# Banded attention and a gated FFN on one core: the fifth block of queries goes over to the 32-query form, in an order of work made anew

## The chip, the cores and the metric

One core of a Trainium2 chip runs the whole program. The metric is device time in microseconds (us), the median of a few executions of the same program. The engines are named as the profile names them: PE is TensorE's matmuls, PEld its weight loads, DVE is VectorE, ACT is ScalarE, POOL is GpSimd, SP is SyncE, which issues nearly all DMAs.

## The reference

The input is q, k, v of shape (8, 8, 576, 64) (batch, heads, sequence, head size) and two weight matrices, 512x2048 and 2048x512, all as drawn in float32 (the weights are handed over as 64-bit numbers).

```
scores = q @ k^T / sqrt(64)             # a query sees its own key and the 63 before it
attn   = softmax(masked scores)         # per head and batch
x      = (attn @ v), heads side by side # 4608 tokens x 512
h      = x @ w_in                       # 4608 x 2048
g      = h if h >= 1, 0 if h <= -1, else (h + 1)^2 / 4
out    = g @ w_out                      # 4608 x 512
```

## The kernel before, in words

**Tiles.** The 4608 tokens are nine tiles of 512 tokens. The attention works in steps of 128 queries (all 8 heads), four steps to a tile, 36 in all; the FFN of a tile loops over 16 blocks f of 128 hidden units. Tiles 0 to 2 are done plainly: `ffn_in` (L1147) makes h in PSUM with three fp32r products (high by high, high by low, low by high), `ffn_relu`, `ffn_square`, `ffn_gate` make g, `ffn_high` and `ffn_low` split it again, `ffn_out` (L1187) adds it to the output. Tiles 3 to 8 are three pairs that share sums of blocks, with seven products in place of eight (`ffn_product` L921, `out_product` L1007). Those pairs read weight sums that `add_sums` (L866) makes beside tiles 1 and 2, and operands that `add_build` (L644) makes from the attention of the pair.

**Weights.** Each block of weights comes as raw 64-bit words by DMA (`w_load`, L304). Five passes on ACT and DVE (L311 to L358) turn it into a high and a low fp32r part. This work fills ACT and DVE through most of tile 0.

**Attention, three forms.** `att_scores` (L426) makes the scores of a step on PE, two PSUM banks.
- Steps 0 to 3 (`PE_MASKS`): 64 queries with 128 keys; PE adds the mask; DVE takes the maximum; ACT takes the exponential; DVE inverts and normalizes; PE transposes (`att_transpose_pe`, L533), eight 128x128 transposes; ACT or DVE copies the two results out of PSUM (`att_transposed`, L539); `att_values` (L542) multiplies by v.
- Step 4 is the same, but DVE adds the mask (L469) and takes the maximum in a second pass (L473).
- Steps 5 and on (s >= `SOON`): 32 queries with 96 keys. `att_masked` (L455) adds the mask and takes the lowest in one pass of eight small instructions (L462); the exponentials are L482; one normalization for both halves (L501); one 32x32-wise transpose on DVE in place (`att_turn`, L506); two DMA writes to the tile moved in DRAM (`att_write`, L517) and one DMA read back into ptd (`att_read`, L521), which leaves the block as `att_values` wants it.

The first step of the last form needs parts of moved to be zero: `att_clear` (L510) on POOL clears a part of ptd, after the values of all steps of the older forms (`early_values`, L627) have been made, since these use the same tile; two DMAs (`att_zero`, L513) write the zeros. There is one such tile ptd for a step (`pt2`) and one moved, so a step's writes wait for the read of the step before, and a step's read waits for the values of the step before.

**The order of the work.** Nothing is ordered by hand, instruction by instruction. Each piece of work is given to `Plan` (L128) with a key, a cost per engine, what it waits for and the buffers that it takes and gives. `Plan.run` goes through the pieces and gives each engine, whenever it is free, the piece that could start first, by least key among those that could (`PATIENCE`, L100, widens this for ACT and POOL). The order that comes out is the program order of each engine and of SP's DMA queue. The keys are in units of one block f for 384 tokens (`step`, L1232; a tile of 512 tokens is 21.33 units). The constants of L33 to L125 set keys and costs: `A_FIRST`, `A_LEAD`, `A_STEP` for the scores, `D_LATE` and `B_DUE` for what follows them, `W_FIRST`, `W_STEP`, `W_LATE` for the weights, `W0_KEY` and `L_LEAD` for loads, `S_LATE` and `S_PACE` for weight sums, `BUILD` for operands. The due times that `soon` (L1235) gives say when a step of tile 1 is wanted. Tile 1 begins with halves of 256 tokens (`FRONT`, L1245): its first half needs steps 4 and 5, its second half steps 6 and 7.

Of the kernel before, what the change touches and what calls it, by code (L numbers as in the profile page):

```python
# [34 lines left out]

PE_STEPS = 5
PE_MASKS = 4
LENT = 2
FIRST = 4
SOON = 5  # L40
JOIN = 8
BEHIND = 2
E_SPAN = 0.29
E_LEAD = 9.81
W_LEAD = -1.5
W_FIRST = (17.22, -2.0, 1.41, 1.48, -3.05)
W_STEP = 1.02
L_LEAD = -0.77
W_LATE = (3.72, -1.06, -2.67, 7.19, 13.28, 13.03, 18.55)
W_LOAD = 1400  # L50
Q_LOAD = 700
K_LOAD = 1040
V_LATE = 2.92
W0_KEY = -100.2
FIRST_LOAD = 0, (0,)
M_LATE = 1
W0_STEP = 12.29
FINE = 4
NWARM = 8
A_FIRST = (-102.6, -95.58, -95.43, -95)  # L60
A_NEXT = 1.57
A_STEP = 4.75
A_SPAN = 2.18
A_LEAD = 4.64
O_LAG = 2.79
O_LAG_DMA = 2300
DMA_LAG = 1300
# [10 lines left out]
B_PE = 2210  # L78
B_DUE = (2.44, -1.28, -0.74)
B_STEP = 5.68  # L80
B_FIRST = 1.45
A_END = 5.86
V_PE = 1270
NORM = dict(Pool=800, DVE=480), dict(DVE=610)
G_LATE = (1.94, 1.65, -4.21, -4.45, 2.08)
D_LATE = (-0.7, 0.46, 6.3, -3.34, 6.37, 0.12)
TURN = 965, 1500
# [5 lines left out]
K_LAG = 4500  # L93
# [4 lines left out]
SUM_KEEP = 1150  # L98
V_LATE_2 = 14.69
PATIENCE = dict(ACT=300, DVE=0, Pool=303, PE=0, SP=0)  # L100
# [5 lines left out]
SUPERS = 3  # L106
H_STEP = 18.67
S_LATE = 1.62
S_PACE = 2.47
O_CHANGE = 3.33, 3.2, 4.7  # L110
EARLY_2 = 2.71
A_SUPER = ((7.71, 2.68), (9.52, 4.03))
A_ORDER = (0, 4, 1, 5, 2, 6, 3, 7)
BUILD = (-12.04, 16.74)
X_SLOTS = 4, 0, 6, 1, 2, 3
# [3 lines left out]
WRITES = (1, None), (2, 1), (0, None), (3, 2), (3, 3), (1, 2), (2, 2)  # L119
R_LEAD = -4.99  # L120
R_LOAD = 430
L_DVE = 4, 6, 8
G_LEAD = (3.99, -2.67, 0.94, -2.12)
OP_LEAD = 10.45
D_LEAD = 0.72  # L125


class Plan:  # L128
# [10 lines left out]
    def add(self, key, cost, do, after=(), takes=(), gives=(), lag=0, shared=False):  # L139
        self.work.append((key, cost, do, set(after), takes, gives, lag, shared))  # L140
        return len(self.work) - 1
# [77 lines left out]
def banded_attention_then_ffn(ctx: ExitStack, tc: tile.TileContext, q, k, v, w, masks, out, out_t, dims):  # L219
# [65 lines left out]
    add = plan.add  # L285
# [76 lines left out]
    def add_weights(f, units):  # L362
        g = f, units
        m = len(units) * DM
        act, high, join, low, small = 105 + .916 * m, 92 + .844 * m, 10 + 1.22 * m, 67 + 1.05 * m, 90 + .25 * m
        key = f * W_STEP - (W_FIRST[f] if f < len(W_FIRST) else W_LEAD) + .5 * units[0]
        x = add(W0_KEY + W0_STEP * (f + .5 * units[0]), dict(SP=W_LOAD * len(units)), lambda e: None if g == FIRST_LOAD else w_load(g), lag=DMA_LAG)
        xr = add(key - W_LATE[0], dict(ACT=act), lambda e: w_rest(g), [x], takes=["u"])
        x = add(key, dict(ACT=act), lambda e: w_sign(g), [xr])
        x = add(key - W_LATE[1], dict(DVE=small), lambda e: w_limit_signed(g), [x])  # L370
        x = add(key - W_LATE[2], dict(DVE=small), lambda e: w_limit_unsigned(g), [x])
        x = add(key - W_LATE[3], dict(DVE=small), lambda e: w_shift(g), [x])
        x = add(key - W_LATE[4], dict(DVE=join), lambda e: w_join(g), [x])
# [294 lines left out]
    def add_step(t, i):  # L668

        s = starts[t] // SB + i  # L670
# [5 lines left out]
        if s < FIRST:  # L676
            key = due = A_FIRST[s]
        elif s >= JOIN:
            key = a_keys[s]
        else:  # L680
            key = a_keys[s]
            due = min(key + A_SPAN, soon(s))
        lk = key - L_LEAD
        apart = A_SUPER[t > PLAIN][1]
        if s == 0:
            last["r"] = add(lk, dict(ACT=480), lambda e: round_masks())
        if s == PE_STEPS - 2:
            last["m"] = add(lk + M_LATE, dict(SP=590), lambda e: load_masks(), lag=DMA_LAG)
        late = s >= JOIN
        xq = add(lk, dict(SP=Q_LOAD), lambda e: load_q(s), takes=["qt"], lag=Q_LAG if late else DMA_LAG)  # L690
        xk = add(lk, dict(SP=Q_LOAD if late else K_LOAD), lambda e: load_k(s) if s else None, takes=["kt"], lag=K_LAG if late else DMA_LAG)
        vk, vl = lk + (V_LATE_2 if late else V_LATE), V_LAG if late else DMA_LAG
# [58 lines left out]
        else:  # L751
            dk = key if s >= JOIN else min(key + E_SPAN, soon(s) - E_LEAD)
            due = [dk + B_DUE[0], dk + B_DUE[0] + B_DUE[2]]
            x = [add(due[h], dict(DVE=LOWEST), lambda e, h=h: att_masked(s, h), [xs, last["m"]], gives=[(ps, xs, h)]) for h in range(2)]
            x = [add(due[h], dict(ACT=EXP[1]), lambda e, h=h: att_exp(s, h, False), [x[h]]) for h in range(2)]
            x = add(due[1], dict(DVE=430), lambda e: att_inverse(s, BOTH), x)
            x = [add(due[1], dict(DVE=870, Pool=1650) if s >= JOIN else dict(DVE=870), lambda e: att_normalize(s, BOTH, e), [x], shared=True)]
            due = dk + B_DUE[1]
            if s == SOON:
# [444 lines left out]
    def out_late(t, q, i):  # L1204
        if t < PLAIN - 1 or q < NF - 2:
            return O_LAG
        return O_CHANGE[0] if q == NF - 2 else O_CHANGE[1 + i // 2]
# [219 lines left out]
```

## Time and profile before

| what | us |
|---|---|
| median of 3 runs | 840.63 (839.79 to 840.87) |
| the profiled execution, its time | 843.4 |
| its span, first to last instruction | 841.6 |
| PE busy in the span | 821.6 |
| DVE busy | 687.0 |
| ACT busy | 533.5 |
| POOL busy | 213.8 |

The profiled execution is one further run of the same program. Its own time is 1.8 us more than its span, which leaves out what lies before the first and after the last instruction, and 2.8 us more than the median of the runs. Its mean granted TensorE clock is 0.994 of 2.4 GHz. Matmul ends are modelled, so two matmuls of a run overlap in the timeline: the cost of one is read from start to start.

### The profile page before, as it was taken

Reading aid. Unit: us, or ns where it says so; the run is one execution under the profiler, and the core shown is the slowest. Engines: PE = TensorE matmul, PEld = TensorE weight load, DVE = VectorE, ACT = ScalarE, POOL = GpSimd, SP = SyncE. Lnnn points to the kernel's source line nnn. Section 1 sums busy time; section 2 is a strip of 40 time slices with the busy share of each in tenths; the row PEclk is TensorE's granted clock in tenths of the full one; section 3 lists DMA queues with packets and bytes.
Section 4 is the critical chain, followed back from the end, with each engine's and each line's share of the span. In section 5 each row is a group of like instructions: output and inputs, shape, how many; then the busy total and the mean of one; then the engine's idle time right before and its main releaser. Section 6 shows DMA issues by size and latency. Waiting matters only on the chain.

```text
span 841.6 us, 18582 instructions
## 1 busy us (share of the span) xinstructions
PE 821.6 (98%) x6588; PEld 672.1 (80%) x6588; DVE 687.0 (82%) x1613; ACT 533.5 (63%) x1303; POOL 213.8 (25%) x226
## 2 busy tenths in 40 slices
PE   7889999999999999999999999999999999999998
PEld 5767788878787878788888888888888888888886
DVE  6999996468757789888899986888999848878964
ACT  5999983545654764756775654777756536566442
POOL 1000014335664636221233320122332201100100
PEclk8999999999999999999999999999999999999999
DMA  8994359996788797788898898888888877777775
GB/s 322 394 375 170 100 165 331 362 331 200 214 265 262 219 285 235 271 252 272 272 333 253 284 316 281 269 268 282 302 252 244 294 230 198 192 195 193 198 224 164
DMA packets 151901, 216.08 MB, mean 257 GB/s; under 512 B 11904, under 2 KB 75264, under 8 KB 151808
## 3 DMA queue, kind: packets, MB, share of 16 engines
q1 hardware_dynamic: 151520, 213.97, 80.2%
q8 instruction: 53, 0.87, 0.4%
q10 hardware_dynamic: 288, 0.92, 0.3%
q14 instruction: 40, 0.33, 0.1%
HBM read 163.72 MB, written 51.12 MB: 255 GB/s over the span
## 4 chain that ended last, share of the span: by engine, by line
PE 75%; DVE 10%; DMA 7%; ACT 3%; issue 2%; POOL 2%; SPq 1%; ACTq 0%; POOLq 0%; DVEq 0%
PE acc L1014 27%; PE ps_h L928 14%; PE acc L928 14%; PE ps_h L1153 8%; PE acc L1199 7%; DMA kept<-u 4%; PE ps_a L439 2%; DVE u L842 1%; PE ps_a L552 1%; DVE u L857 1%; PE ps_h L552 1%; DVE u L849 1%; DMA raw<-in_w 1%; DVE wts L358 1%; DMA kt<-in_k 1%
## 5 line engine op out<-in xcount | busy, mean ns | idle before, releaser
L1014 PE MATMUL acc<-op,wts 128*128 128x512 f32 x576 | 137.7, 390 | 0.0
L1153 PE MATMUL ps_h<-xh,wts 128*128 128x512 f32 (+1 forms) x424 | 131.2, 376 | 6.1 <-DVE a L1175 4.4
L290 ACT CAST op<-g 128x512 fp32r<-128x512 f32 x129 | 80.2, 622 | 77.4 <-PE acc L1014 49.3
L1014 PEld LDWEIGHTS acc<-op,wts 128*128 128x128 f32 x576 | 107.8, 188 | 22.5
L1199 PE MATMUL acc<-wts,gh 128*128 128x512 f32 x384 | 120.1, 394 | 0.7 <-ACT gh L1180 0.7
L482 ACT ACTIVATE sm<-sm,nm 128x96 f32<-128x96 f32 x248 | 89.5, 363 | 12.3 <-DVE nm L462 11.6
L1153 PEld LDWEIGHTS ps_h<-xh,wts 128*128 128x128 f32 x424 | 78.0, 190 | 22.6 <-DVE a L1175 6.5
L1005 DVE TENSOR_TENSOR op<-g,op 128x512 fp32r<-128x512 f32 x107 | 76.7, 718 | 20.7 <-ACT op L290 20.2
L928 PE MATMUL ps_h<-wts 128*128 128x512 f32 x360 | 92.0, 391 | 0.0
L928 PE MATMUL acc<-wts 128*128 128x512 f32 x360 | 91.5, 389 | 0.0
L1199 PEld LDWEIGHTS acc<-wts,gh 128*128 128x128 f32 x384 | 70.8, 188 | 16.0 <-ACT gh L1180 1.1
L1168 ACT ACTIVATE a<-a 128x512 f32<-128x512 f32 (+1 forms) x125 | 77.1, 617 | 3.8
L1153 PE MATMUL ps_h<-xl,wts 128*128 128x512 f32 (+1 forms) x212 | 78.8, 372 | 0.6 <-DVE xl L565 0.6
L928 PEld LDWEIGHTS acc<-wts 128*128 128x128 f32 x360 | 67.5, 188 | 14.2
L928 PEld LDWEIGHTS ps_h<-wts 128*128 128x128 f32 x360 | 67.2, 188 | 14.2
L1199 PE MATMUL acc<-wts,gl 128*128 128x512 f32 x192 | 75.3, 392 | 1.4 <-DVE gl L1185 1.4
L1163 ACT ACTIVATE a<-g 128x512 f32<-128x512 f32 x96 | 60.5, 630 | 19.4 <-DVE g L943 14.0
L1175 DVE SCALAR_TENSOR_TENSOR g<-a,g 128x512 f32<-128x512 f32 x96 | 68.1, 716 | 3.8 <-ACT a L1168 3.2
L1005 POOL TENSOR_TENSOR op<-g,op 128x512 fp32r<-128x512 f32 x28 | 36.1, 1295 | 129.5 <-ACT op L290 118.1
L1185 POOL TENSOR_TENSOR gl<-a,gh 128x512 fp32r<-128x512 f32 (+1 forms) x34 | 48.6, 1429 | 45.0 <-ACT gh L1180 43.2
L992 DVE TENSOR_TENSOR g<-g 128x512 f32<-128x512 f32 x83 | 58.4, 717 | 0.5
L1175 DVE SCALAR_TENSOR_TENSOR a<-a,ps_h 128x512 f32<-128x512 f32 (+1 forms) x53 | 33.3, 628 | 25.1 <-ACT a L1168 24.9
(145 smaller groups left out, 1544.5 us busy)
## 6 DMA issues: line engine op xcount, KB each, us to landing
wts<-kept SPq DMA_DIRECT2D x240, 256.0 KB, 3.6
vt<-in_v SPq DMA_DIRECT2D x72, 256.0 KB, 4.9
ptd<-moved SPq DMA_DIRECT2D x31, 512.0 KB, 4.7
kt<-in_k SPq DMA_DIRECT2D x35, 384.0 KB, 5.1
kept<-wts SPq DMA_DIRECT2D x48, 256.0 KB, 4.8
gh<-kept SPq DMA_DIRECT2D x48, 256.0 KB, 3.7
gl<-kept SPq DMA_DIRECT2D x48, 256.0 KB, 3.6
raw<-in_w SPq DMA_DIRECT2D x12, 1023.8 KB, 10.6
```

The costliest lines, as they stand in the source:

```text
L290: nc.scalar.copy(dst, src)
L482: nc.scalar.activation(t, t, AF.Exp, bias=nm[:, g:g + 1], scale=-1.0, accum_out=den[:, g:g + 1])
L928: nc.tensor.matmul(ps, lhsT=r[:, part, cp], rhs=x_op(k, xp)[:, cp], start=j in (0, 1, 3, 4) and i == 0 and cp == 0, stop=j in (1, 2, 5, 6) ...
L992: engine[eng].tensor_tensor(out=g[:, out], in0=g[:, a], in1=g[:, b], op=op)
L1005: engine[eng].tensor_tensor(out=low, in0=g_of(n)[:, of], in1=high.bitcast(F32), op=ALU.subtract)
L1014: nc.tensor.matmul(opened[b][m], lhsT=r[:, part, m], rhs=op[xp], start=j in (0, 1, 3, 4) and i == 0 and n == 0, stop=j in (1, 2, 5, 6) and ...
L1153: nc.tensor.matmul(ps, lhsT=wts[f, 0][:, part, c * P:(c + 1) * P], rhs=x[:, c, r], start=(c == 0 and j == 0), stop=(c == NP - 1 and j == 2),)
L1163: nc.scalar.activation(gs[t, f, r.start][0], phs[t, f, r.start], AF.Relu, bias=0.5, scale=0.5)
L1168: nc.scalar.activation(a, a, AF.Square)
L1175: nc.vector.scalar_tensor_tensor(out=ps if t >= PLAIN else a, in0=a, scalar=1.0, in1=ps, op0=ALU.min, op1=ALU.max)
L1185: engine[eng].tensor_tensor(out=g[2], in0=g[0], in1=g[1].bitcast(F32), op=ALU.subtract)
L1199: nc.tensor.matmul(acc[t, i][:, n], lhsT=g[:, sub], rhs=wts[f, 1][:, part, n], start=(q == 0 and j == 0), stop=(q == NF - 1 and j == 2 and ...
```

## The change

Step 4 goes over to the form of steps 5 and on: `PE_STEPS` and `SOON` are 4 in place of 5. So its scores are 32 smaller products in place of 16, the second maximum pass, the eight PE transposes and the two copies fall away, and one DVE transpose, two DMA writes and one DMA read are added. `att_clear` and `att_zero` belong to step 4 now and wait for the values of steps 0 to 3; the mask load belongs to step 2. The constants of the order are new throughout, and some have new companions: `A_SHIFT` moves the due times of steps 0 to 7 one by one, `L_LEAD_1` and `B_DUE_1` stand for the steps before step 8, `O_LAG_1` for tile 0; `AHEAD` puts the first q load, the first k load and the first weight load ahead of all others (the last two are issued from ACT already).

```diff
@@ -33,36 +33,40 @@
 FRONT = 2
 BACK = 1
 
-PE_STEPS = 5
+PE_STEPS = 4
 PE_MASKS = 4
 LENT = 2
 FIRST = 4
-SOON = 5
+SOON = 4
 JOIN = 8
 BEHIND = 2
-E_SPAN = 0.29
-E_LEAD = 9.81
-W_LEAD = -1.5
-W_FIRST = (17.22, -2.0, 1.41, 1.48, -3.05)
-W_STEP = 1.02
-L_LEAD = -0.77
-W_LATE = (3.72, -1.06, -2.67, 7.19, 13.28, 13.03, 18.55)
+E_SPAN = 6.84
+E_LEAD = 3.34
+W_LEAD = -1.6
+W_FIRST = (15.88, -1.61, 3.35, 3.69, -1.83, -1.49, -1.81, -2.17, -1.35, -1.5, -1.09, -0.24, -0.95, -2.54)
+W_STEP = 1.23
+L_LEAD = 0.75
+L_LEAD_1 = -2.65
+W_LATE = (5.04, -3.82, -1.64, 5.78, 15.71, 7.97, 16.52)
 W_LOAD = 1400
 Q_LOAD = 700
 K_LOAD = 1040
-V_LATE = 2.92
-W0_KEY = -100.2
+V_LATE = 5.42
+W0_KEY = -104.03
 FIRST_LOAD = 0, (0,)
-M_LATE = 1
-W0_STEP = 12.29
+M_LATE = 4.03
+AHEAD = -10000
+W0_STEP = 12.28
 FINE = 4
 NWARM = 8
-A_FIRST = (-102.6, -95.58, -95.43, -95)
-A_NEXT = 1.57
-A_STEP = 4.75
-A_SPAN = 2.18
-A_LEAD = 4.64
-O_LAG = 2.79
+A_FIRST = (-106.83, -104.6, -94.45, -93.06)
+A_SHIFT = (-5.96, -4.16, -2.18, 1.29, -0.01, 2.05, -4.27, 2.83)
+A_NEXT = 2.2
+A_STEP = 5.3
+A_SPAN = 20.93
+A_LEAD = 0.18
+O_LAG = 3.7
+O_LAG_1 = 1.81
 O_LAG_DMA = 2300
 DMA_LAG = 1300
 BEGIN = dict(PE=1500, ACT=2300, DVE=2500, SP=2400)
@@ -76,14 +80,15 @@
 EXP = 1545, 1440
 S_PE = 1230, 1150
 B_PE = 2210
-B_DUE = (2.44, -1.28, -0.74)
-B_STEP = 5.68
-B_FIRST = 1.45
-A_END = 5.86
+B_DUE = (-1.05, 0.05, 0.26)
+B_DUE_1 = (2.86, 0.39, -3.32)
+B_STEP = 6.97
+B_FIRST = 1.97
+A_END = 4.22
 V_PE = 1270
 NORM = dict(Pool=800, DVE=480), dict(DVE=610)
-G_LATE = (1.94, 1.65, -4.21, -4.45, 2.08)
-D_LATE = (-0.7, 0.46, 6.3, -3.34, 6.37, 0.12)
+G_LATE = (3.58, -0.41, 1.25, -3.23, 0.31)
+D_LATE = (4.19, 2.68, 7.36, 5.5, 3.95, 1.1)
 TURN = 965, 1500
 HOP_SP = 690, 460
 HOP_LAG = 3300, 5500
@@ -96,7 +101,7 @@
 STORE_LAG = 3500
 SUM_PASS = 1950
 SUM_KEEP = 1150
-V_LATE_2 = 14.69
+V_LATE_2 = 20.53
 PATIENCE = dict(ACT=300, DVE=0, Pool=303, PE=0, SP=0)
 BUFS = dict(qt=2, kt=2, vt=4, ps_a=2, sm=2, ptd=3, pt2=1, x=2, u=2, ps_h=2, a=2, gh=2, gl=2, acc=4, o=2, tmp=2)
 BUFS.update({n: 1 for n in ("xtmp", "xs0", "xs1", "xs2", "xs3", "xs4", "xs5", "X", "Y")}, raw=4, ring=7, op=5)
@@ -104,25 +109,25 @@
 
 PLAIN = 3
 SUPERS = 3
-H_STEP = 18.67
-S_LATE = 1.62
-S_PACE = 2.47
+H_STEP = 18.73
+S_LATE = -4.94
+S_PACE = 3.38
 O_CHANGE = 3.33, 3.2, 4.7
-EARLY_2 = 2.71
-A_SUPER = ((7.71, 2.68), (9.52, 4.03))
+EARLY_2 = 1.41
+A_SUPER = ((9.97, 3.21), (9.61, 4.57))
 A_ORDER = (0, 4, 1, 5, 2, 6, 3, 7)
-BUILD = (-12.04, 16.74)
+BUILD = (12.11, 14.5)
 X_SLOTS = 4, 0, 6, 1, 2, 3
 G_FIRST = 8
 RING_SLOT = 7
 PARTS = (0, 0, 0), (1, 1, 1), (0, 5, 4), (1, 3, 2), (0, 4, 3), (1, 6, 5), (0, 2, 6)
 WRITES = (1, None), (2, 1), (0, None), (3, 2), (3, 3), (1, 2), (2, 2)
-R_LEAD = -4.99
+R_LEAD = -10.46
 R_LOAD = 430
 L_DVE = 4, 6, 8
-G_LEAD = (3.99, -2.67, 0.94, -2.12)
-OP_LEAD = 10.45
-D_LEAD = 0.72
+G_LEAD = (4.38, -2.41, 0.86, 1.43)
+OP_LEAD = 14.06
+D_LEAD = 11.82
 
 
 class Plan:
@@ -364,7 +369,7 @@
         m = len(units) * DM
         act, high, join, low, small = 105 + .916 * m, 92 + .844 * m, 10 + 1.22 * m, 67 + 1.05 * m, 90 + .25 * m
         key = f * W_STEP - (W_FIRST[f] if f < len(W_FIRST) else W_LEAD) + .5 * units[0]
-        x = add(W0_KEY + W0_STEP * (f + .5 * units[0]), dict(SP=W_LOAD * len(units)), lambda e: None if g == FIRST_LOAD else w_load(g), lag=DMA_LAG)
+        x = add(W0_KEY + W0_STEP * (f + .5 * units[0]) if g != FIRST_LOAD else AHEAD + 2, dict(SP=W_LOAD * len(units)), lambda e: None if g == FIRST_LOAD else w_load(g), lag=DMA_LAG)
         xr = add(key - W_LATE[0], dict(ACT=act), lambda e: w_rest(g), [x], takes=["u"])
         x = add(key, dict(ACT=act), lambda e: w_sign(g), [xr])
         x = add(key - W_LATE[1], dict(DVE=small), lambda e: w_limit_signed(g), [x])
@@ -674,21 +679,25 @@
         pt, pv = ("ps_h", "acc") if s < LENT else ("ps_a", "ps_a")
         ps = "acc" if s < FIRST and s % 2 else "ps_a"
         if s < FIRST:
-            key = due = A_FIRST[s]
+            key = A_FIRST[s]
+            due = key + A_SHIFT[s]
         elif s >= JOIN:
             key = a_keys[s]
         else:
             key = a_keys[s]
-            due = min(key + A_SPAN, soon(s))
-        lk = key - L_LEAD
+            due = min(key + A_SPAN, soon(s)) + A_SHIFT[s]
+        lk = key - (L_LEAD if s >= JOIN else L_LEAD_1)
         apart = A_SUPER[t > PLAIN][1]
         if s == 0:
             last["r"] = add(lk, dict(ACT=480), lambda e: round_masks())
         if s == PE_STEPS - 2:
             last["m"] = add(lk + M_LATE, dict(SP=590), lambda e: load_masks(), lag=DMA_LAG)
         late = s >= JOIN
+        if s == 0:
+            lk = AHEAD
         xq = add(lk, dict(SP=Q_LOAD), lambda e: load_q(s), takes=["qt"], lag=Q_LAG if late else DMA_LAG)
-        xk = add(lk, dict(SP=Q_LOAD if late else K_LOAD), lambda e: load_k(s) if s else None, takes=["kt"], lag=K_LAG if late else DMA_LAG)
+        xk = add(lk + (s == 0), dict(SP=Q_LOAD if late else K_LOAD), lambda e: load_k(s) if s else None, takes=["kt"], lag=K_LAG if late else DMA_LAG)
+        lk = key - (L_LEAD if s >= JOIN else L_LEAD_1)
         vk, vl = lk + (V_LATE_2 if late else V_LATE), V_LAG if late else DMA_LAG
         xv = add(vk, dict(SP=Q_LOAD), lambda e: load_v(s, 0), last["v"], takes=["vt"], lag=vl)
         xw = add(vk, dict(SP=Q_LOAD), lambda e: load_v(s, 1), [xv], takes=["vt"], lag=vl)
@@ -749,13 +758,14 @@
                 ready.append(x)
             gives = [("ptd", taken[0]), ("ptd", taken[1])]
         else:
-            dk = key if s >= JOIN else min(key + E_SPAN, soon(s) - E_LEAD)
-            due = [dk + B_DUE[0], dk + B_DUE[0] + B_DUE[2]]
+            dk = key if s >= JOIN else min(key + E_SPAN, soon(s) - E_LEAD) + A_SHIFT[s]
+            late_by = B_DUE if s >= JOIN else B_DUE_1
+            due = [dk + late_by[0], dk + late_by[0] + late_by[2]]
             x = [add(due[h], dict(DVE=LOWEST), lambda e, h=h: att_masked(s, h), [xs, last["m"]], gives=[(ps, xs, h)]) for h in range(2)]
             x = [add(due[h], dict(ACT=EXP[1]), lambda e, h=h: att_exp(s, h, False), [x[h]]) for h in range(2)]
             x = add(due[1], dict(DVE=430), lambda e: att_inverse(s, BOTH), x)
             x = [add(due[1], dict(DVE=870, Pool=1650) if s >= JOIN else dict(DVE=870), lambda e: att_normalize(s, BOTH, e), [x], shared=True)]
-            due = dk + B_DUE[1]
+            due = dk + late_by[1]
             if s == SOON:
                 z = add(due - 2, dict(Pool=600), lambda e: att_clear(), early_values)
                 last["d"] = [add(due - 2, dict(SP=HOP_SP[0]), lambda e, j=j: att_zero(j), [z], lag=HOP_LAG[0]) for j in range(2)]
@@ -1203,7 +1213,7 @@
 
     def out_late(t, q, i):
         if t < PLAIN - 1 or q < NF - 2:
-            return O_LAG
+            return O_LAG if t else O_LAG_1
         return O_CHANGE[0] if q == NF - 2 else O_CHANGE[1 + i // 2]
 
     os = {}
```

## Rows read from the trace of the kernel before

**Rows 1.** This is the profile page, parts 1 and 2, whole span: the span; busy time of each engine, its share of the span and its instructions; the TensorE clock granted in 40 equal slices, in tenths of full speed.

```profile
span 841.6 us, 18582 instructions
PE 821.6 (98%) x6588; PEld 672.1 (80%) x6588; DVE 687.0 (82%) x1613; ACT 533.5 (63%) x1303; POOL 213.8 (25%) x226
...
PEclk8999999999999999999999999999999999999999
```

**Rows 2.** This is busy time by stretches, whole core: stretch (us from the start of the span), its length, busy time and instructions of PE, PEld, DVE, ACT and POOL, mean granted TensorE clock (1.00 is 2.4 GHz), mean busy share of the DMA engines, GB/s.

```profile
0.00:10.00 10.00, 6.97 (x73) 5.74 (x77) 3.90 (x10) 4.24 (x11) 2.91 (x16) 1.00 0.77 275
10.00:20.00 10.00, 7.24 (x97) 5.72 (x89) 8.70 (x25) 7.26 (x33) 0.00 (x0) 0.66 1.01 360
20.00:30.00 10.00, 7.74 (x93) 6.76 (x91) 8.63 (x26) 9.39 (x40) 0.00 (x0) 0.83 1.02 368
30.00:60.00 30.00, 26.07 (x281) 20.77 (x279) 28.54 (x70) 28.56 (x56) 0.00 (x0) 1.00 0.99 386
60.00:120.00 60.00, 59.84 (x522) 47.97 (x523) 59.29 (x142) 57.45 (x125) 0.30 (x1) 1.00 0.43 152
300.00:346.00 46.00, 43.34 (x428) 34.50 (x431) 39.55 (x115) 27.10 (x80) 24.04 (x22) 1.00 0.77 233
346.00:842.00 496.00, 492.04 (x3462) 404.44 (x3451) 411.17 (x868) 297.61 (x679) 94.94 (x82) 1.00 0.81 253
```

**Rows 3.** This is who waited for whom, PE alone, whole span: what waited, for which engine's line; us in total, times, longest.

```profile
PE ps_h L1153 <- DVE a L1175: 4.4, 6, 1.6
PE ps_h L537 <- DVE den L493: 1.7, 1, 1.7
PE ps_h L1153 <- DVE xh L292: 1.7, 1, 1.7
...
PE acc L1199 <- DVE gl L1185: 1.4, 3, 0.9
```

**Rows 4.** This is the timeline of the first 10 us, SP's DMA issues and then PE: start us, us, engine, line, operation, tiles, count [idle before and its releaser].

```profile
1.19 0.42 SPq L417 DMA_DIRECT2D vt<-in_v  x1
...
2.12 0.71 SPq L411 DMA_DIRECT2D kt<-in_k  x1
...
9.40 1.10 PE L439 MATMUL acc<-kt,qt 64*64 64x128 f32 x32 [1.57 <-DMA kt<-in_k]
```

**Rows 5.** This is the timeline of PE from 45 to 66 us, columns as in the group before: the scores of step 4 (64x128), those of step 5 (64x96), and the first four transposes of step 4, each with the work behind it.

```profile
45.87 1.10 PE L439 MATMUL ps_a<-kt,qt 64*64 64x128 f32 x32
46.90 0.50 PE L1153 MATMUL ps_h<-xh,wts 128*128 128x512 f32 x1
...
51.20 1.00 PE L439 MATMUL ps_a<-kt,qt 64*32 64x96 f32 x64
52.13 0.73 PE L1199 MATMUL acc<-wts,gh 128*128 128x512 f32 x2
53.72 0.50 PE L1199 MATMUL acc<-wts,gl 128*128 128x512 f32 x1 [0.86 <-DVE gl L1185]
...
65.07 0.60 PE L537 MATMUL ps_a<-idt,sm 128*128 128x128 f32 x4
65.42 0.48 PE L1153 MATMUL ps_h<-xh,wts 128*128 128x512 f32 x1
65.74 0.40 PE L1153 MATMUL ps_h<-xl,wts 128*128 128x512 f32 x1
```

**Rows 6.** This is the instructions on the tile sm from 44 to 76 us (steps 4 and 5), then the copies of transposed blocks on ACT (0 to 140 us) and the one of step 4 on DVE: line, engine, operation, tiles, count: duration in ns, least, median, longest; start of the first and the last; shapes. The last row is one of the timeline.

```profile
L486 ACT ACTIVATE sm<-sm,nm x8: 385/386/399, 52.1 to 68.7; 128x128 f32<-128x128 f32 x8
L462 DVE CUSTOM_DVE_ANT_0 sm<-ps_a,nmsk x8: 226/242/252, 54.2 to 60.7; 128x96 f32<-128x96 f32 x8
L482 ACT ACTIVATE sm<-sm,nm x8: 357/359/370, 60.4 to 62.9; 128x96 f32<-128x96 f32 x8
L501 DVE TENSOR_TENSOR sm<-sm,den x3: 674/684/930, 62.4 to 70.3; 128x512 f32<-128x512 f32 x2, 128x768 f32<-128x768 f32 x1
L469 DVE SCALAR_TENSOR_TENSOR sm<-ps_a,msk x2: 668/670/673, 47.4 to 48.0; 128x512 f32<-128x512 f32 x2
L473 DVE TENSOR_REDUCE nm<-sm x2: 669/670/670, 49.2 to 49.8; 128x4 f32<-128x512 f32 x2
L508 DVE STREAM_TRANSPOSE sm<-sm x1: 959/959/959, 68.5 to 68.5; 128x768 f32<-128x768 f32 x1
...
L290 ACT COPY ptd<-ps_a x5: 584/586/587, 29.6 to 73.3; 128x512 f32<-128x512 f32 x5
...
66.14 0.67 DVE L292 COPY ptd<-ps_a 128x512 f32<-128x512 f32 x1
```

**Rows 7.** This is the transfers of the tile moved from 0 to 140 us (L519 writes it, L522 reads it back), columns as in the group before, their time from issue to landing, and GpSimd's wait ahead of its clearing of ptd (columns as in group 3).

```profile
L519 SPq DMA_DIRECT2D moved<-sm x8: 590/610/633, 78.5 to 130.4; - x8
...
DMA to landing us min/median/max: 2.1/3.4/4.6
...
POOL ptd L511 <- ACT a L1163: 71.7, 1, 71.7
```

**Rows 8.** This is the timeline around step 7: its scores on PE, the issue that reads its turned block back, its values on PE (columns as in group 4).

```profile
103.02 1.00 PE L439 MATMUL ps_a<-kt,qt 64*32 64x96 f32 x64
...
122.33 0.38 SPq L522 DMA_DIRECT2D ptd<-moved  x1
...
132.59 1.15 PE L552 MATMUL ps_a<-ptd,vt 128*64 128x64 f32 x32
```

## The prediction

> **What bounds the kernel now.** I read the page first: PE is busy 821.6 of 841.6 us [rows 1], so 20.0 us of idle PE is all that any order could give back, beside the time at half clock and work taken off PE itself. Then the busy time by stretches, for where the 20.0 lie [rows 2]: 3.03 + 2.76 + 2.26 = 8.05 before 30 us, 3.93 from 30 to 60, 0.16 from 60 to 120, 2.66 from 300 to 346, and 3.96 from 346 on (0.4 of them past the end of the span); 1.6 are left for 120 to 300. The reader is to see three regimes. Before 30 us PE waits for the first attention steps, at a granted clock of 0.66 and 0.83. From 30 to 120 us DVE (28.54 of 30, 59.29 of 60) and ACT (28.56 and 57.45) are as full as PE, and to 60 the DMA engines too (0.99). From 346 on PE alone binds, and nothing that the change touches lies there. The waits of PE [rows 3] then name who is late: DVE nearly always. So what the change takes off PE counts in full wherever it lies, what it takes off DVE and ACT counts where PE waits for them, before 60 us, and a later time of any step costs only if PE runs out of other work.
>
> **PE's own work.** The four transposes of a half take 65.42 - 65.07 = 0.35 us from start to start [rows 5]; two halves go: -0.7. The scores go from 46.90 - 45.87 = 1.03 to 52.13 - 51.20 = 0.93: -0.1. The values keep their number of products. Sum -0.8, on the path, since PE binds after 60 us and step 4 is transposed at 65 us.
>
> **DVE and ACT.** DVE drops two mask passes and two maxima of 0.670, two normalizations of 0.684 and one copy of 0.67 (the other half's copy fell to ACT): 4.72 us. It takes on eight mask pieces of 0.242, one normalization of 0.930 and the transpose of 0.959: 3.83 [rows 6]. One of two inversions goes as well; I count nothing for it. So -0.9 on DVE. ACT saves 8 x (386 - 359) ns = 0.2 and one copy of 0.59: -0.8. Worth on the path: nothing at the least (from 60 to 120 PE is idle for 0.16 only), -1.7 at the most, if both pass on in full into the 3.93 us of 30 to 60. The masks and maxima of step 4 stand at 47.4 to 50 us on DVE, shortly ahead of the gl for which PE waits 0.86 at 53.72 [rows 5, 6]; that part alone shrinks from 2.68 to 1.94. I take -0.7, nearest to that row.
>
> **The three transfers.** Two writes of 0.61 us each on SP and one read, 2.1 to 4.6 us to landing [rows 7]. What hides them: the values of step 4 are wanted by the first half of tile 1, and step 7's values, still later in that row of four, come at 132.59 [rows 8]; with step 4's scores at 45.87 there is room for tens of us. Cost 0; with that cover gone, two landings in a row, up to 9.2. All steps 4 to 7 now share one ptd and one moved, a trip more in the chain; at 10 us or less for a trip, four of them fit between 65 and 130. The clearing on POOL, which sat waiting 71.7 us [rows 7], waits for step 3's values only and comes some 40 us earlier. Its two zero writes then fall among the weight loads, where the DMA engines are full: no longer than two L519 issues, 1.2 us, hidden by weights that ACT and DVE take up much later than they land; bounds 0 and +1.2, I take 0. So is the mask load one step earlier, an issue of 0.71 or less like the k load's [rows 4].
>
> **The order made anew, first 30 us.** Step 1's q and k are issued ahead of step 0's v now. Before, the v issue at 1.19 stood ahead of k at 2.12, and PE waited 1.57 us for that k [rows 4]: some 0.4 to be had there. Behind it PE waits 1.7 for DVE's den, then 1.7 for the first xh [rows 3]; the due times of steps 0 to 2 are earlier by `A_SHIFT`. Bounds: all 8.05 us of idle gone, or a further wait of 1.7 of the kind seen. Nothing in the trace shows the new sequence. I take -0.5, near the one row that has a direct answer.
>
> **The order made anew, 130 to 346 us.** Weight sums begin earlier and are spread wider (first key 22.95 to 16.39, last 60.0 to 67.1 units), operand builds rank later (`BUILD` -12.04 to 12.11). DVE has 6.45 of 46 us free from 300 to 346, and POOL 22 [rows 2], which hides a different sequence. Bounds: the 2.66 us of idle there gone, or doubled. I take 0.
>
> **Sum.** -0.8 - 0.7 - 0.5 = -2.0. The profiled execution spans 841.6 us and takes 843.4, so 839.6 and 841.4 for one like it. It stands 2.8 above the median of the runs; against that, 840.63 - 2.0 = **838.6**.
>
> **Rival 1: nothing on the path but PE's work, or not even that.** In its favour: from 60 to 120 us PE is idle for 0.16 us only, so lighter DVE and ACT there only free buffers sooner; before 60 the new order may spend the room on other work. Against it: PE waits on DVE at 53.72. Time: 839.8, and 840.6 if the 0.8 comes back as a wait.
>
> **Rival 2: step 7 comes too late, slower than before.** By `A_LEAD` its scores had the key 21.33 - 4.64 = 16.69; now they follow step 8's key of 24.16 at a distance of 5.3, key 18.86. A unit is 24 products of 384 columns, 3.8 us at 2.4 GHz, so 2.17 units are 8.3 us. The scores came at 103.02, the read was issued 19.3 us later, and the values were made at 132.59 [rows 8]. From 103.0 + 8.3 - 2.0 = 109.3 on the same chain issues the read at 128.6 and lands, with at most 4.6 more [rows 7], at 133.2, where PE wants it at 130.6. Its mask and maximum are due at 20.95 + 2.86 = 23.8 units, behind the start of tile 1 at 21.33, on a DVE with 0.7 us free of 60 [rows 2]: left lying until then, some 9.5 us late. It decides from a landing past 130.6; what is queued behind the values on PE is the second half of tile 1 and its gates. Price between 2.6 and 9.5; I take 5: 843.6. Against it: the last trip had some 6 us to spare, PE can draw step 8's scores and further products of the first half ahead, and a due time only ranks what is ready.
>
> The Trainium skill speaks against the change at the same place: its page "VectorE: DVE Perf Modes", section "Rules for kernel authors", gives a 128x128 transpose to TensorE wherever PSUM will do as its target. By that rule the -0.7 for the transposes would not be a gain, and the sum would be 839.3. The rows show the rule's half: on PE a half is turned in 0.35 us, far sooner than through DRAM, but its two copies take more of ACT and DVE (0.59 and 0.67) than the one turn of 0.959.
>
> **Rival 3: the front gains far more.** Granted 0.66 and 0.83 [rows 2], PE ran about 6.8 and 3.4 us of 10 to 30 us at the lower of its two levels, 1.2 GHz; the idle pieces of 10 to 30 us lie among these. If the first FFN products come 4 us earlier, half of the 8.05, the time is 834.6. Against it: the chain of four steps on ACT, with exponentials for each, stays as it is.
>
> **How the numbers follow.** About 0.2% (1.7 us: 838.95 and 842.3) is what a measurement can tell from no change. Forecast 0.52, with its own range 836 to 840.3 (0.42 of it below 838.95, 0.10 above). Rival 1 0.18, all within. Rival 2 0.24, 0.23 of it past 842.3. Rival 3 0.06. So faster 0.48, same 0.29, slower 0.23. The range of 835.2 to 843.8 leaves out most of rival 3 (0.05) and the upper half of rival 2 (0.12); it takes in the bounds of DVE, the zero writes and the sums singly.
>
> **What would show it.** Right: no L537 and no copies to ptd after 45 us; L508 once more; the idle of PE from 30 to 60 at 3.2 or less; from 0 to 30 at 7.5; L522 of step 4 landing long before its values; 346 to the end unchanged. Wrong: a wait of PE for the values or xh of step 7 near 130 us (rival 2); idle from 30 to 60 still at 3.9 (rival 1); a first L1153 well ahead of before (rival 3); new waits from 150 to 346 would overturn the 0 that I took for sums and builds.

## The result: slower by 1.0%, and the profile after

The kernel after takes 848.15 us (median of 4 runs, 847.49 to 851.36), the kernel before 840.21 (4 runs, 839.72 to 840.87): a ratio of 1.0102, 95% interval 1.0075 to 1.0128. The ratios here and below are taken over all runs; that of the two medians can differ by 0.001 (here it is 1.009). 838.6 was forecast, 843.8 was the upper end.

The page of the kernel after, part 1 [rows 1]: PE has 24 instructions more and 25.8 us idle where it had 20.0.

```profile
span 849.1 us, 18648 instructions
PE 823.3 (97%) x6612; PEld 671.7 (79%) x6612; DVE 687.5 (81%) x1617; ACT 539.0 (63%) x1312; POOL 206.5 (24%) x221
```

Busy time by stretches of the kernel after, columns as in [rows 2].

```profile
0.00:10.00 10.00, 6.58 (x81) 5.57 (x84) 3.11 (x8) 3.40 (x6) 2.93 (x16) 1.00 0.77 271
10.00:20.00 10.00, 6.13 (x70) 4.68 (x66) 9.13 (x26) 9.54 (x40) 0.00 (x0) 0.66 1.05 414
20.00:30.00 10.00, 8.27 (x130) 6.79 (x122) 9.69 (x27) 9.08 (x39) 0.00 (x0) 1.00 0.96 361
30.00:60.00 30.00, 25.07 (x304) 20.48 (x304) 29.16 (x83) 29.45 (x65) 0.30 (x1) 1.00 0.96 377
60.00:120.00 60.00, 60.00 (x521) 48.18 (x520) 59.47 (x146) 54.79 (x119) 0.00 (x0) 1.00 0.55 189
120.00:150.00 30.00, 29.36 (x177) 24.52 (x176) 17.93 (x36) 12.67 (x24) 12.50 (x16) 1.00 0.94 282
150.00:160.00 10.00, 6.90 (x87) 4.73 (x86) 2.87 (x5) 5.19 (x10) 4.81 (x6) 0.83 1.09 378
160.00:300.00 140.00, 140.00 (x1391) 114.19 (x1390) 98.06 (x317) 85.82 (x260) 78.26 (x88) 1.00 0.81 254
300.00:346.00 46.00, 42.52 (x435) 34.24 (x433) 38.67 (x101) 25.16 (x70) 22.09 (x23) 0.93 0.78 231
```

The reader is to see two places that are new: from 150 to 160 us PE is idle for 3.10 and its granted clock is 0.83 (in the kernel before 10.00 busy at 1.00), and from 300 to 346 the clock is 0.93. PE's waits [rows 3] name them, in rows two and four.

```profile
PE ps_h L1163 <- DVE a L1185: 3.6, 4, 1.3
PE ps_a L557 <- DMA ptd<-moved: 3.5, 1, 3.5
PE ps_h L542 <- DVE den L498: 3.2, 1, 3.2
PE acc L1209 <- ACT gh L1190: 3.0, 1, 3.0
```

**The first new wait** goes back through three in-order queues. SP's DMA issues of the kernel after, then ACT, then PE (timeline, columns as in [rows 4]):

```profile
140.37 0.72 SPq L871 DMA_DIRECT2D kept<-o  x1
...
143.37 5.26 SPq L834 DMA_DIRECT2D kept<-wts  x6
148.72 1.14 SPq L1237 DMA_DIRECT2D out<-o  x2
```

```profile
137.17 0.62 ACT L295 CAST o<-u 128x512 fp32r<-128x512 f32 x1
...
146.53 0.59 ACT L295 COPY o<-acc 128x512 f32<-128x512 f32 x1 [3.07 <-DMA kept<-o]
153.06 0.59 ACT L295 COPY o<-acc 128x512 f32<-128x512 f32 x1 [5.94 <-DMA out<-o]
153.54 0.41 ACT L1190 CAST gh<-a 128x256 fp32r<-128x256 f32 x1
```

```profile
150.60 0.39 PE L1209 MATMUL acc<-wts,gl 128*128 128x512 f32 x1
154.00 0.73 PE L1209 MATMUL acc<-wts,gh 128*128 128x512 f32 x2 [3.02 <-ACT gh L1190]
...
158.90 1.00 PE L444 MATMUL ps_a<-kt,qt 64*32 64x96 f32 x64
```

Read from the bottom: PE waits for gh; gh stands on ACT behind an output copy; the copy waits 5.94 us for one of the two buffers o; that buffer is free when its store, issued at 148.72, has landed, 4.3 us later. The copy behind that store came late itself (146.53 to 147.12): it had waited 3.07 us for a buffer that a weight sum's high part held. ACT had cast that part into o at 137.17, its store (kept<-o, L871) was issued at 140.37 and landed 6.1 us later. Of the 5.94 us, SP's place for the output store, behind six stores of weight sums (L834, 5.26 us of issuing), is 1.6 (147.12 to 148.72).

The kernel before has the same hold on ACT, 5.75 us, at no cost. Stores of weight sums ahead of the output's are not new either, it has nine of them; but its two buffers are free for the outputs from 140.42 on, no cast of a sum lies between. SP of the kernel before, then ACT, then PE:

```profile
138.27 7.00 SPq L824 DMA_DIRECT2D kept<-wts  x9
145.37 1.14 SPq L1227 DMA_DIRECT2D out<-o  x2
```

```profile
140.42 0.57 ACT L290 COPY o<-acc 128x512 f32<-128x512 f32 x1
...
150.44 0.59 ACT L290 COPY o<-acc 128x512 f32<-128x512 f32 x1 [5.75 <-DMA out<-o]
150.92 0.41 ACT L1180 CAST gh<-a 128x256 fp32r<-128x256 f32 x1
```

```profile
151.56 0.39 PE L1153 MATMUL ps_h<-xh,wts 128*128 128x512 f32 x1
151.79 0.61 PE L1199 MATMUL acc<-wts,gh 128*128 128x512 f32 x2
```

There gh is done at 150.92 + 0.41 = 151.33 and wanted at 151.79, behind products of h that need nothing from ACT: 0.46 us of room (0.22 to the weight load on PEld that reads it, at 151.56), which no table of idle PE shows. In the kernel after the hold ends 2.6 us later (153.06), and PE's order has drawn its products of h ahead (the last starts at 147.88): out products alone follow up to the scores at 158.90.

**The second new wait**: the writes of a turned block are issued from 305.58 on and have landed at 310.56; the read is issued 0.5 us behind that, at 311.07, and takes 8.6 us to land. SP, the landing times of the three (tile moved, 305 to 312 us), then PE, then the stretches around both waits, of the kernel after:

```profile
305.58 1.32 SPq L524 DMA_DIRECT2D moved<-sm  x2
...
311.07 0.38 SPq L527 DMA_DIRECT2D ptd<-moved  x1
```

```profile
DMA to landing us min/median/max: 4.1/4.3/8.6
```

```profile
319.81 1.97 PE L557 MATMUL ps_a<-ptd,vt 128*64 128x64 f32 x32 [3.48 <-DMA ptd<-moved]
```

```profile
150.00:155.00 5.00, 1.90 (x8) 0.97 (x7) 0.50 (x1) 1.92 (x5) 1.65 (x4) 0.98 1.09 387
155.00:160.00 5.00, 5.00 (x80) 3.76 (x81) 2.37 (x5) 3.27 (x6) 3.15 (x3) 0.68 1.09 368
315.00:320.00 5.00, 1.52 (x10) 0.97 (x10) 5.00 (x10) 1.85 (x3) 3.15 (x3) 0.87 0.39 148
320.00:325.00 5.00, 5.00 (x40) 4.21 (x39) 2.22 (x6) 1.10 (x2) 0.00 (x0) 0.50 0.83 208
```

After each wait PE runs at a granted clock of 0.68 and 0.50 for a stretch, so a wait costs more than its own length. This profiled execution took 851.36 us, the other three of its runs 847.5 to 848.2; a second profiled execution (c1 below, 847.48) has the first wait again (3.2), and the second as 1.9 only, at full clock, behind a read that landed in 7.0. So the first is in both, and the full size of the second is not; why that read took 8.6 is not shown.

### The profile page after: what moved, and what is told of

Same layout as the page of the kernel before. It is cut to its first block, busy times and chain, and to the rows that moved or that the text cites. A ratio compares the mean times of both kernels' runs of the same rounds, so it can differ in the third digit from the quotient of the medians.

```text
span 849.1 us, 18648 instructions
## 1 busy us (share of the span) xinstructions
PE 823.3 (97%) x6612; PEld 671.7 (79%) x6612; DVE 687.5 (81%) x1617; ACT 539.0 (63%) x1312; POOL 206.5 (24%) x221
## 4 chain that ended last, share of the span: by engine, by line
PE 83%; DVE 8%; DMA 4%; issue 2%; ACT 1%; POOL 1%; SPq 0%; ACTq 0%; POOLq 0%
PE acc L1024 27%; PE acc L938 13%; PE ps_h L938 13%; PE acc L1209 12%; PE ps_h L1163 11%; PE ps_a L444 3%; PE ps_h L557 1%; DMA kept<-u 1%; DVE wts L363 1%; PE ps_a L557 1%; PE acc L557 1%; DMA ptd<-moved 1%; DVE raw L328 1%; DMA raw<-in_w 1%; DVE u L351 1%
## 5 line engine op out<-in xcount | busy, mean ns | idle before, releaser
L1209 PE MATMUL acc<-wts,gh 128*128 128x512 f32 x384 | 122.7, 401 | 3.0 <-ACT gh L1190 3.0
L1015 DVE TENSOR_TENSOR op<-g,op 128x512 fp32r<-128x512 f32 x117 | 85.0, 733 | 22.2 <-ACT op L295 21.6
L487 ACT ACTIVATE sm<-sm,nm 128x96 f32<-128x96 f32 x256 | 92.4, 364 | 4.3 <-DVE nm L467 3.6
L1209 PEld LDWEIGHTS acc<-wts,gh 128*128 128x128 f32 x384 | 72.5, 192 | 19.3 <-ACT gh L1190 3.4
L1195 POOL TENSOR_TENSOR gl<-a,gh 128x512 fp32r<-128x512 f32 (+1 forms) x34 | 46.4, 1367 | 49.9 <-ACT gh L1190 42.1
L1002 DVE TENSOR_TENSOR g<-g 128x512 f32<-128x512 f32 x84 | 56.4, 696 | 0.3
L467 DVE CUSTOM_DVE_ANT_0 sm<-ps_a,nmsk 128x96 f32<-128x96 f32 x256 | 48.1, 250 | 10.0 <-PE ps_a L444 10.0
L1173 ACT ACTIVATE a<-ps_h 128x512 f32<-128x512 f32 (+1 forms) x53 | 29.3, 552 | 40.8 <-PE ps_h L1163 40.6
```

The costliest lines, as they stand in the source:

```text
L467: nc.vector.tensor_tensor_reduce(out=sm[:, :, g], in0=ps[:, p].rearrange("p (c n) -> p c n", n=SQ), in1=m, scale=-scale, scalar=3.0e38, op ...
L487: nc.scalar.activation(t, t, AF.Exp, bias=nm[:, g:g + 1], scale=-1.0, accum_out=den[:, g:g + 1])
L1002: engine[eng].tensor_tensor(out=g[:, out], in0=g[:, a], in1=g[:, b], op=op)
L1015: engine[eng].tensor_tensor(out=low, in0=g_of(n)[:, of], in1=high.bitcast(F32), op=ALU.subtract)
L1173: nc.scalar.activation(gs[t, f, r.start][0], phs[t, f, r.start], AF.Relu, bias=0.5, scale=0.5)
L1209: nc.tensor.matmul(acc[t, i][:, n], lhsT=g[:, sub], rhs=wts[f, 1][:, part, n], start=(q == 0 and j == 0), stop=(q == NF - 1 and j == 2 and ...
```

## The experiments

Where a time is lost is read from progress: the start of the n-th FFN product of tiles 0 to 2 in each trace, counted from the timeline, as the difference in us to e12 (which is the kernel before with one more buffer o, and the trace of the old order that was undisturbed at the front). PE's attention work is not in the count. From product 360 on every column has the same amount of it behind it, but for the change's own 24 instructions and for e4 and e10 at 1080 (32 instructions more); at 180 the new orders have 32 more.

| product | before, as profiled | c0 | after, as profiled | c1 | e3 | e4 | e10 | e5 |
|---|---|---|---|---|---|---|---|---|
| 0 (23.79 us) | 1.5 | 0.8 | 0.3 | 0.3 | 0.3 | 0.0 | -0.2 | -0.3 |
| 180 (73.5) | 2.3 | 2.5 | -0.4 | -1.0 | -1.1 | -1.2 | -1.5 | -1.4 |
| 360 (120.6) | 2.4 | 2.5 | 0.0 | -0.6 | -0.7 | -0.8 | -1.1 | -1.0 |
| 468 (141.3) | 2.4 | 2.5 | 1.3 | 0.6 | 0.6 | 1.0 | 0.8 | -0.8 |
| 576 (168.0) | 2.4 | 2.9 | 6.6 | 5.6 | 3.4 | 2.2 | 1.2 | -0.8 |
| 1080 (306.1) | 2.1 | 1.8 | 4.6 | 3.6 | 1.2 | 1.9 | 1.6 | 1.4 |
| span (838.8) | 2.8 | 1.9 | 10.3 | 6.4 | 2.2 | 1.3 | 2.1 | 8.1 |

**c0_before, c1_after**: both kernels unchanged, for their spread.

> The kernel before, unchanged, for a second trace of it beside the others of this chip. If the first trace of before was typical: block 0 of the pairs again begins near 346.4 us and 10 us of the first 30 run at 1.2 GHz. If it was a late one: block 0 begins near 342.6 (its usual span of 837.8 less the 495.2 us of the pairs), with less time at 1.2 GHz before 30 us or without the 1.6 us wait at 312.9.

> The kernel after, unchanged, a second trace. Theory A1: the first stall (PE waits for gh behind a late output store on ACT near 151 us, 3 us, then half clock) is there again, since it follows from the program order. The second one (3.5 us for the read of ptd at 316 us) is open: with it some 849 us of span, without it 845 to 846.

Measured: before against itself 840.34 to 840.31, ratio 1.0002 (0.9988 to 1.0017), single runs from 838.4 to 843.1; after 847.47, 1.0087 (1.0067 to 1.0106). The difference is real, 7.2 us here; single traces of the kernel before can't be trusted to 2 us.

**e1_form_alone, e2_order_alone**: the two halves of the change.

```diff
# e1: kernel before            # e2: kernel after
-PE_STEPS = 5                  -PE_STEPS = 4
+PE_STEPS = 4                  +PE_STEPS = 5
-SOON = 5                      -SOON = 4
+SOON = 4                      +SOON = 5
```

> The kernel before with PE_STEPS = 4 and SOON = 4 alone, all constants of its order kept (the planner lays the order anew from about 45 us on with them). Theory A (the two stalls at 151 and 316 us come from the new constants): 838.5 to 840.5, some 0 to 1.7 us faster than before, PE idle from 120 to 346 us at 5 or less. Theory B (they come from the fifth step's form, its transfers and lighter DVE work): 845 or more, with waits of 3 us near 150 and 316 us.

> The kernel after with PE_STEPS = 5 and SOON = 5, so step 4 in the old form under the new constants. Theory A: 846 to 850, a stall of 3 us or more of PE between 145 and 160 us remains. Theory B: 839 to 842, no such stall.

Measured: 852.84, 1.0158 (1.0139 to 1.0176), and 857.56, 1.0214 (1.0195 to 1.0233), with 839.75 for before. Each half is worse than the whole, so their prices don't add. In both the planner lays the order anew (in e1 from about 45 us on). In e1 PE is idle for 5.4 us from 60 to 150 us and waits 5.5 for the gh that is read back at 360; in e2 it waits 4.5 for xh, 3.8 for ptd<-moved and 1.9 for o between 120 and 165. What follows: neither run prices "the form" or "the order"; each prices another order.

**e3_third_o, e4_sums_old**: e3 keeps the order of the kernel after and gives every third of the first 24 requests for a buffer o a third one; e4 puts the weight sums back to their old keys.

```diff
# e3
...
+    if len(o_count) <= 24 and len(o_count) % 3 == 0:
+        return const.tile(shape, F32, name="oh", tag="lent")
...
# e4
-S_LATE = -4.94
-S_PACE = 3.38
+S_LATE = 1.62
+S_PACE = 2.47
```

> The kernel after, program order of every engine the same; the first 24 requests for the tile o (output stores of the plain tiles, high parts of weight sums) go round three buffers in place of two (the third is the tile lent by the masked steps). Theory A1 (at 151 us ACT waits for a late output store to give o back, and PE waits for the gh queued behind that on ACT): the 5.9 us wait of ACT is 1 us or less, PE's 3.0 at 154 is gone and the clock of 155 to 160 us stays 1.00, 4 to 5 us faster than after: 843 to 844.5. Rival A2 (gh would be late anyway, since the full DMA queue or the gate's own chain holds it): the wait of PE stays at 2 us or more, 847 to 849.

> The kernel after with S_LATE and S_PACE of before alone: weight sums begin later and end earlier. Theory A1 (stores of sums ahead of the output stores in SP's queue make the first stall): first stall gone or below 1 us, 842 to 845. Second stall open: if the sums' stores also delay the read at 311 us it goes too, 839.5 to 841.5. Rival (sums have no part in it): 847 to 849.

Measured: e3 844.52, 1.0058 (1.0041 to 1.0076); e4 843.38, 1.0045 (1.0027 to 1.0062). In e3, with no instruction moved, the wait for gh falls from 3.0 to 1.2 us, no clock is lost behind it (1.00 from 150 to 160), and the second wait is 1.6, at full clock (1.9 in c1). ACT still waits 4.0 for a buffer, where 1 or less was expected, but that ends at 147.26. e4 waits 1.1 for gh; there the sum's cast comes behind the output copies, which have both buffers. Both take the loss where the table has it, between products 468 and 576: 5.0 in c1, 2.8 in e3, 1.2 in e4.

**e10_third_o_sums_old, e12_before_third_o**: both mends together, and the buffer in the kernel before.

> Kernel after with both single mends: every third of the first 24 requests for a buffer o goes to a third one, and S_LATE 1.62, S_PACE 2.47 are those of before. Theory A (both runs lost at one place, o buffers held by late stores): the mends overlap, so that with the sums already in their old place a third buffer adds at most 1 us: 842.5 to 844, ratio to before 1.002 to 1.005. Rival (two separate losses, 2.7 % of a per cent and more each): they add up, 3.0 + 4.1 us off after's 847.5: 840.4, ratio 1.000.

> Kernel before with the third buffer o alone (every third of the first 24 requests). Theory A: before does not lose time at its o buffers, so nothing changes, 839.8 to 841, ratio 0.999 to 1.001. Rival (the buffers cost before too, so e3's gain says nothing of the change): 3 us, 837.5, ratio 0.996 to 0.998.

Measured: e10 843.65, 1.0039 (1.0026 to 1.0051), no better than e4 alone; e12 839.78, 0.9996 (0.9987 to 1.0005), against 840.13. So the old order did not pay for its o buffers, and the two mends act at one place: of the 5.0 us between products 468 and 576, 0.4 are left in e10. By the times alone it is not shown that they don't add, since each difference between two of these ratios is uncertain by some 2 us. By the ratios (1.0087 less 1.0058, 1.0045 and 1.0039, of 840) 2.4 to 4.0 of the 7.2 us, each give or take those 2, come from the chain of sum's cast, buffer o and copy on ACT.

**e9_stores_act**: the same chain cut at SP: ACT issues tile 0's output stores.

```diff
-nc.sync.dma_start(out=out[r:r + P, n], in_=os[t, i][:, n])
+(nc.scalar if t == 0 else nc.sync).dma_start(out=out[r:r + P, n], in_=os[t, i][:, n])
```

> The kernel after with the four output stores of tile 0 issued by ACT, where the result is copied, in place of SP; nothing else moved. Theory A1 (these stores stand on SP behind stores of weight sums that the new S_LATE brought forward): they are issued within 1 us of their copy, ACT's wait for o falls below 2 us and PE's wait for gh near 154 us below 1 us: 842.5 to 845, as e3. Rival A2 (the DMA engines are full, so the stores land late wherever they are issued): PE waits 2 us or more there, 846.5 to 848.5.

Measured: 848.00 against 841.10, 1.0091 (1.0077 to 1.0106). The wait for gh shrinks to 1.4, yet ACT still waits 3.9 for the buffer and a wait of 2.3 for DVE follows by product 648. Nothing is left of it at the end. The stores did leave SP, but the two buffers were still held: one by the sum's store (issued on SP at 139.37, landed 6.8 us later), one by the first output store, which DVE's copy had ready at 136.74 and which ACT, in its own order, issued at 140.01 (landed 5.9 us later). So SP's place is not the only one in the chain, the landing and the sum's cast are others.

**e5_late_old, e6_sums_steps_old**: the kernel after with all constants of the later stages as before (sums, builds, steps of the pairs, ring loads), and with those of the sums and of the pairs' steps alone (`S_LATE`, `S_PACE`, `A_SUPER`).

> The kernel after with those constants of before that rank work after tile 0: V_LATE_2, H_STEP, S_LATE, S_PACE, EARLY_2, A_SUPER, BUILD, R_LEAD, G_LEAD, OP_LEAD, D_LEAD, B_DUE, B_STEP, B_FIRST, A_END, O_LAG. PE's order is that of after for its first 692 instructions. Theory A (the front of after is good, its later order bad): 836 to 840, below or at before. Theory C (any order laid anew that was not tuned as a whole makes stalls): 845 or more, with waits of PE past 346 us, as in e1 and e2.

> The kernel after with S_LATE, S_PACE and A_SUPER of before: weight sums as in e4, and the attention steps of the pairs later again. Theory A: first stall as small as in e4 and no second one, 839 to 842. Theory C: 845 or more.

Measured: 848.51, 1.0100 (1.0074 to 1.0126), and 849.73, 1.0115 (1.0095 to 1.0135). e5 has no loss at 150 us and stays ahead of e12 up to product 576, then loses 2.2 up to product 1080 (waits of 1.5 and 1.6 at 262 and 305 us) and 6.7 behind it, most of it at the handover to the pairs, as theory C had it. SP, then PE, then the stretches, of e5:

```profile
348.76 1.06 SPq L1237 DMA_DIRECT2D out<-o  x2
...
350.42 0.45 SPq L918 DMA_DIRECT2D gh<-kept  x1
```

```profile
354.76 2.90 PE L938 MATMUL acc<-wts,gh 128*128 128x512 f32 x6 [5.04 <-DMA gh<-kept]
```

```profile
350.00:355.00 5.00, 0.24 (x1) 0.27 (x2) 4.34 (x23) 3.49 (x17) 0.00 (x0) 0.87 0.98 315
355.00:360.00 5.00, 5.00 (x12) 3.86 (x13) 1.26 (x2) 1.85 (x3) 0.00 (x0) 0.50 1.03 383
```

The load that PE needs first stands on SP behind two output stores that wait for their data: the same pattern, at another place. e6 waits 5.38 at the same load.

**e7_late_old_ring, e8_form_ring**: e5 and e1 with the first of these ring loads, those into gh and gl, issued by POOL, past SP.

```diff
...
+eng = nc.gpsimd if s > 4 and s not in ring_slots else nc.sync
...
-nc.sync.dma_start(out=r.bitcast(F32), in_=kept[l][n][:, PARTS[j][1]])
+eng.dma_start(out=r.bitcast(F32), in_=kept[l][n][:, PARTS[j][1]])
```

> e5 (the front of after, the later constants of before) with the first weight loads into gh and gl for the pairs issued by POOL in place of SP; every other instruction and every order as in e5. In e5 they stood on SP behind two output stores and a write of moved, were issued at 350.4 us, and PE waited 5.0 us for gh, then ran at half clock: 11.5 us in all between block 0 and the end. Theory D (that place in SP's queue is the whole loss of e5): the wait is gone, block 0 to the end takes 495 to 497, the time is 836 to 839, some 2 to 4 us faster than before. Rival (the load is late for the full DMA engines, not for its place): the wait stays at 2 us or more, 843 or more.

> e1 (the new form of step 4 under the constants of before) with the same loads issued by POOL. Theory D: the 5.5 us wait goes, 841 to 844, what is left over before being the stalls of 60 to 150 us that its newly laid order has; so the form alone gains nothing. Rival: 850 or more.

Measured: e7 844.83 against 841.10, 1.0050 (1.0038 to 1.0063); e8 851.79, 1.0126 (1.0106 to 1.0146). e7 has its load issued at 342.19 and gives back about half of e5's loss; PE then waits 2.3 at 355.07 for the next load in line, wts<-kept, which was left on SP behind the same two output stores (issued at 350.54, landed 4.4 us later). So the place in SP's queue is the loss there, as theory D said, but moving two loads of it gave neither its time nor a wait below 2. e8 gains little on e1, whose loss lies mostly earlier.

**e11_lag_6000**: the planner is told that an output store takes 6.0 us.

```diff
-O_LAG_DMA = 2300
+O_LAG_DMA = 6000
```

> Kernel after with O_LAG_DMA 6000 in place of 2300: the planner reckons that an output store takes 6.0 us to land (out<-o was seen at 2.2, 4.2 and 6.1). It changes the order from PE's 905th piece of work on. Theory A (the order is blind to how late the stores are): the wait for gh behind the o copy at about 154 us and its like go, 843 to 845, ratio 1.003 to 1.006. Rival (any re-laid order of this program makes another stall elsewhere, as e5 and e6 did): the wait at 154 us goes or shrinks, but a wait of 3 us or more turns up where none was, 847 to 852, ratio 1.008 to 1.014.

Measured: 852.05, 1.0141 (1.0126 to 1.0157). The wait at 154 us is gone, and PE waits 3.6 for DVE's a at 173.78 and 2.5 for wts at 350.00 instead. The rival holds: a truer cost of one transfer does not make a better order.

## Why the prediction was wrong, point by point

**PE's own work, -0.8.** The operations did change as said: no transposes of step 4 are left (32 of L542 in place of 40) and its scores are of the 96-key kind. Its size can't be read off by itself, since waits at half clock raise PE's busy time (818.7 in e12, 821.9 in c1).

**DVE and ACT, -0.7.** Not confirmed. The instructions cost what was taken from [rows 6] or up to 5% more; on the tile sm of the kernel after, from 40 to 80 us:

```profile
L467 DVE CUSTOM_DVE_ANT_0 sm<-ps_a,nmsk x24: 221/254/259, 45.1 to 76.1; 128x96 f32<-128x96 f32 x24
...
L506 DVE TENSOR_TENSOR sm<-sm,den x2: 952/955/958, 55.5 to 70.1; 128x768 f32<-128x768 f32 x2
L513 DVE STREAM_TRANSPOSE sm<-sm x2: 972/974/976, 57.8 to 73.0; 128x768 f32<-128x768 f32 x2
```

But PE's idle from 30 to 60 us grew from 3.93 to 4.93 where 3.2 or less was to be seen: its waits for DVE's a in that stretch are 3.6 now, 1.0 before. The wait for gl at 53.72, which the -0.7 was read from, is gone; the new order has put others in its place.

**The three transfers, 0.** Right for steps 4 to 7: step 4's values come at 78.8, 21 us after its turn at 57.8, and step 7's earlier than before, not later [rows 8]. PE of the kernel after:

```profile
85.55 1.00 PE L444 MATMUL ps_a<-kt,qt 64*32 64x96 f32 x64
...
123.38 1.15 PE L557 MATMUL ps_a<-ptd,vt 128*64 128x64 f32 x32
```

So rival 2, the slow one that I named, did not happen: its scores came at 85.55, not 109.3. A key ranks what is ready; I had read it as a time.

**The first 30 us, -0.5.** The wait for k was 0.79 in c1 and 1.52 in the other trace of the kernel after; in the old order it was 1.57, 1.59 and, in c0, 0.96, so no gain is shown. PE's wait for den grew from 1.7 to 3.2. Idle PE from 0 to 30 us, 7.5 by the forecast, was 9.02 and 7.75. The first FFN product starts at 24.09 and 24.04, against 25.30, 24.60 and 23.79 in three traces of the old order. The sum forecast up to this place, -2.0, is -2.4 to -3.1 at product 360 against the two profiled executions of the kernel before, and 0.0 to -0.6 against e12. That it comes near -2.0 is luck as far as the terms go, since the difference between these is clock, which no term counts: with the same program order on PE, e12 was granted 1.00 from 10 to 30 us where [rows 2] have 0.66 and 0.83 (its busy time by stretches):

```profile
10.00:20.00 10.00, 6.91 (x136) 5.20 (x127) 8.95 (x27) 8.77 (x36) 0.00 (x0) 1.00 1.01 362
20.00:30.00 10.00, 6.92 (x100) 5.43 (x92) 9.79 (x28) 9.73 (x41) 0.00 (x0) 1.00 1.03 417
```

e12's front is the rare kind: of the 48 runs of the kernel before that stand beside the experiments, 36 had a mean clock of 0.996 or less, as the two profiled ones (0.994), with a median of 840.5 us, and 12 had 0.997 or more (838.9); e12's trace has 1.000.

**The order made anew, 130 to 346 us: 0.** This is the step that failed. It measured +7.0 in c1 against e12 (from -0.6 at product 360 to 6.4 at the end): +1.2 up to product 468, +5.0 from there to 576, -2.0 up to 1080 (e12 has 1.9 us of waits there that c1 has not), +2.8 behind that, with the second wait in it. The pairs have next to no part in it: from their first product to the end the kernel after takes 495.3 and 496.3 us, the old order 495.2 to 495.8 in three traces. I hid a different sequence behind free time of DVE and POOL, and bounded it by the idle that PE had there (2.66 gone or doubled). Neither says anything on an in-order queue. What set the time at the largest of these losses was two buffers o, the landing of their stores (4.3 to 6.1 us) and ACT's place for a copy; the room in the kernel before was 0.46 us at 151.33. An order that starts the sums earlier (first key 22.95 to 16.39, which I had noted) puts a sum's cast into o ahead of the output copies; with the old keys (e4) it comes behind them. The last sentence of the prediction named such waits from 150 to 346 us as what would overturn the 0; no rival gave them a price or a chance.

**What stays open.** With both mends e10 is still 3.5 us behind before. In the traces PE is idle for 4.4 us from 120 to 360 in e10, at several small waits (the longest 1.1), and for 2.5 (c0), 3.2 (e12) and 4.3 (the first trace) in the old order, so idle PE does not account for it. Nor is it shown why the new front gains so little: PE's longer wait for den may be one reason, and ten of the eleven traces with this front were granted 0.66 to 0.68 from 10 to 20 us (e7 0.83), but neither was tried by itself.

## What to carry to other kernels

Where an order is laid by a planner, a changed key or cost is a new program: price it by the in-order queues, and look in the trace of before for the holds that cost nothing yet (an engine that waits long for a store, with a hand-off queued behind it) and how little room they have. The 2.0 us that were forecast from work saved and a better front are less than one hold that comes to light, wait and low clock together (5.0). Half a change under constants fitted to the whole, or to the other half, is no price for that half.

## What the runs showed of the hardware that was not expected

Output stores of tile 0 landed in 3.3 to 5.1 us (c1, four of them, DMA engines at 1.08), much as in the kernel before (3.4 to 5.0), and one read of a turned block in 8.6. The 2.1 to 4.6 of [rows 7], which the prediction took for such transfers, end at 140 us: from 280 to 330 us the reads of the kernel before land in 4.8 to 6.7. And equal waits do not cost equal clock: the same front, with waits of 1.0 to 1.7 us, was granted 0.66, 0.83 and 1.00 from 10 to 20 us in three executions of the old order, which alone moves its first 72 products by 2.4 us; waits of 1.2 at 153 us (e3) and 1.9 at 317 (c1) cost no clock, a wait of 2.3 at 189 (e9) was followed by 0.66 over the next 5 us, waits of 3.0 to 5.0 by 0.50 to 0.84.
